# Batches 1 to 3 in stretches of 512 columns, and a new order of work behind the opening

## The chip, the cores and the metric

The kernel runs on one core of a Trainium2 chip. The metric is the device time of one execution in microseconds, as the median of several runs. The core has five engines that run side by side, each with its own queue of instructions in a fixed order: TensorE (PE in the profile; PEld is its loading of weights), VectorE (DVE), ScalarE (ACT), GpSimd (POOL), and SyncE (SP), which here only issues transfers.

## The reference

The input is q, k and v of four batches with four heads, 1088 positions and 32 features a head, two small matrices S1 and S2 of 8 x 32, and four weights. First comes an attention without softmax:

```
phi(x)  = outer(S1 x, S2 x) flattened to 64 features      (for every position and head)
kv      = sum over positions of phi(k) v^T                 (64 x 32)
z       = sum over positions of phi(k)
x       = phi(q) kv / (phi(q) z + 1e-6)                    (heads side by side: 1088 x 128)
```

Then two mixing steps, in float32 throughout:

```
h   = relu(x^T @ w_tok1) @ w_tok2        over positions: 1088 -> 256 -> 1088
u   = x + h^T
out = u + relu(u @ w_ch1) @ w_ch2        over channels:  128 -> 1536 -> 128
```

## The kernel before

**Splitting for accuracy.** A wide product of batches 1 to 3 and every channel product is made from three fast ones: each operand is cut into a high and a low part (`uh` and `ul`, `hh` and `hl`, the two `halves` of a weight), and high x high, high x low and low x high are added up in one PSUM bank. The weights arrive as 64-bit words that ACT, DVE and GpSimd turn into such halves in the opening.

**Stages.** For each batch b the keys' features and sums are made (`K<b>`: `.p` projects, `.c` copies, `.v` multiplies, `.s` sums over positions into a bank, `.kvz` copies that out). The queries' features are made by `Q<b>`; for batches 1 to 3 they go through DRAM (`.p`, `.c`, four writes `.w`, six broadcasting reads `.r`, then four multiplications `.m`). `A<b>` is the attention and the mixing over positions: `.x` the attention's matmuls (line 692), `.n`, `.r`, `.d` the division, `.h` and `.l` the split of x, `.t` the first product (line 758), `.relu`, `.hT` the transpose, `.w` the second product (line 878), `.xb`, `.xm` and `.xT` the transposition of x by way of DRAM, `.us` their sum u, `.uh` and `.ul` its split (lines 849 and 852).

**The channel mix.** All columns (positions of all batches, one after another) are cut into stretches, listed in `SPANS`: three for batch 0 and nine for batches 1 to 3, seven of 384 columns, one of 320 and one of 256. Stretch i has twelve blocks of 128 hidden channels. A block is four steps in the function `channel_mix`: `U<i>.f` (three matmuls into a bank of `ps_h`, line 928), `U<i>.h` (ACT's relu into `hh`, line 932), `U<i>.l` (DVE's low part into `hl`, line 935), and `U<i>.s` (three matmuls that add to the stretch's bank of `ps_o`, line 941). After the twelfth block `U<i>.ol` adds u (line 960 for batch 0, line 966 for the others) and `U<i>.out` stores the result from SP (line 977). A stretch that crosses from one batch to the next has two stores.

**The order.** Nothing is decided at run time. `ORDER` is a list of step names, written out by hand ahead of time; `Plan.run` emits the steps in that order, each into the queue of its engine (`@pool` and `@dve` choose one where there are several). `~n` stands for n matmuls on zeros that only keep PE occupied in the opening. Every step lies behind the earlier ones of its engine, and waits for the semaphores of what it reads.

**Buffers.** Each kind of tile rotates through a fixed number of buffers, given in `bufs` (line 223). The n-th tile of a kind takes buffer n modulo that number, once all readers of the tile that was there are done. Of the eight PSUM banks three are `ps_a`, three `ps_h` and two `ps_o`. `HID` = 4 buffers hold `hh` and `hl`, so that four blocks can stand between the first and the second product.

Of the kernel before, what the change touches and what calls it, by code (L numbers as in the profile page):

```python
# [89 lines left out]
w10.lo@pool U1.f U1.h U1.l U1.s U1.s w04.lo@pool U1.s A1.n0 U2.f U2.f k2 v2 A1.r0 A1.d0 q3 A1.n2 A1.r2 U1.h A1.n1  # L90
A1.r1 U1.l A1.d2 A1.d1 U1.s A1.xb A1.xm U2.f U2.h w11.hi U2.l K2.p U2.s k3 U2.h U2.l U2.h A1.xT0 K2.c0 K2.c8 U2.l
U2.f U2.f K2.c4 K2.v0 K2.v8 U2.s U2.f K2.v4 w14.lo@pool U2.s A1.xT1 A1.xT2 w12.hi Q2.p U2.h U2.h A1.h0 K2.s
w12.lo@dve A1.l0@pool U2.h Q2.c0 A1.h2 A1.h1 Q2.c1 A1.l2@dve A1.l1@dve U2.l Q2.w0 Q2.w3 w11.lo@dve w15.lo@dve K3.p
K2.kvz Q2.w2 A1.t0 U2.l U2.l U1.ol Q2.w1 K3.c4 A1.t1 A1.t2 K3.c0 A1.xT3 U2.s U1.out Q2.r0None K3.v0 U2.f Q2.r00
A1.relu A1.hT K3.v4 Q2.r01 U2.h Q2.r1None K3.c8 U2.l U2.s U2.f U2.h A1.hTh Q2.r10 U2.l U2.s U2.f U2.f A1.hTl Q2.r11
U2.f v3 U2.s U2.s K3.v8 A1.w0 U2.h U2.l U2.h U2.l A1.us0 U2.oh@dve U2.s A1.w1 A1.us1 A1.w2 A1.us2 U2.h U2.l A1.uh03
A1.uh14 U2.f U2.h U2.s U2.l A1.ul03@pool U3.f U2.s U3.f U3.f U3.h U3.l U3.f U3.h U3.l U2.s U3.s U3.f U3.h U3.h U2.ol
U3.l Q2.m00@dve U3.s U3.s U3.f U3.h U3.h A1.uh25 U3.l U3.s U3.f U3.h U3.l U3.f A1.ul25@pool U3.l U3.s U3.s U3.f U3.h
U3.l U3.h U3.f U3.s U3.h U3.l U3.l U3.f U3.l U3.h Q2.m01@dve U3.s U3.s U3.s Q2.m11@dve Q2.m10@dve U3.f U3.h U3.l
A1.ul14@pool U4.f U4.h A2.x A2.n2 A2.n0 U3.l U4.l A2.r0 A2.r2 A2.n1 U3.s A2.d0 A2.h0 U4.f U4.h U4.f A2.d2 A2.r1  # L100
A2.d1 A2.xb U4.l A2.l0@pool A2.h1 A2.xm K3.s A2.h2 A2.l2@dve Q3.p Q3.c0 Q3.c1 Q3.w0 Q3.w1 Q3.w3 Q3.w2 A2.l1@dve U3.s
U4.f U4.s A2.xT0 A2.xT1 U4.f A2.xT2 U4.s A2.xT3 U4.h U4.l U4.h Q3.r0None Q3.r00 Q3.r01 K3.kvz A2.t0 Q3.r1None Q3.r10
A2.t1 A2.t2 A2.relu U4.f U4.s U4.h A2.hT A2.hTh U4.l U4.l A2.hTl U4.f U4.s U4.s U4.h U4.l U4.f U4.f A2.w0 A2.w1 U4.h
U4.l U4.s U4.s U4.h U4.l U4.h U4.f U4.h U4.f U4.h A2.us0 A2.uh06 A2.uh05 A2.us1 U4.l U4.s A2.w2 A2.uh17 A2.uh16 U4.l
A2.ul05@pool U4.s U2.out A2.ul16@pool U4.f U4.h U5.f U4.s A2.us2 A2.uh27 A2.uh28 U4.l A2.ul06@pool U4.l U5.f U4.s
U5.f U4.s U5.h U5.h U5.l U5.f U5.h Q3.m00@pool U5.h Q3.r11 U5.l U3.ol U3.out U5.s U5.f U5.s U5.l U5.f U5.h U5.l U5.f
U5.l U5.f U5.s U5.s U5.s U5.h U5.l U5.f U5.h U5.l U5.f U5.s U5.s U4.ol U5.h U5.l U5.f U5.s U5.h U5.l U5.s
A2.ul17@pool U5.h U5.h U5.l U5.f U6.f U5.h U5.s U5.l U5.l Q3.m10@dve U6.f U5.s U5.s U6.f Q3.m11@pool U6.h U6.h
A2.ul27@dve U6.h U6.l U6.f Q3.m01@pool U6.h U6.s U6.l U6.l U6.s U6.f U6.h U6.f U6.h A3.x A3.n0 A3.n1 U6.l U6.l U6.l
U6.s A3.r1 A3.r0 A3.n2 A3.d0 A2.ul28@pool A3.h0 A3.d1 A3.l0@dve A3.h1 U6.s U6.s U5.ol U5.out U6.f U6.f U6.h U6.l  # L110
U6.f U6.s U6.s A3.r2 A3.d2 A3.h2 U6.f U6.h A3.xb U5.out A3.t0 A3.l2@dve A3.l1@pool U6.l U6.h A3.t1 U6.s U6.h A3.t2
U6.f U6.h A3.relu U6.l U6.f U6.s U6.h U6.l U7.f U6.s U6.l U6.l A3.hT A3.hTh U7.f U7.f U7.h A3.hTl U7.h U7.l U6.s
U6.s U7.f U7.l A3.w0 A3.w1 U7.f U7.s U7.s U7.h U7.h U7.h U7.l U7.l U7.s A3.w2 U7.f U7.h U7.f U7.s U7.h A3.xm A3.xT0
A3.xT1 A3.xT2 U7.l U7.f A3.xT3 A3.us0 A3.uh08 A3.ul08@pool A3.us1 U7.l U7.l U7.s A3.uh09 U7.f U7.s U7.f A3.uh110
U7.h A3.us2 U7.l U7.s A3.ul09@dve U7.h U7.l U7.s A3.ul110@dve A3.uh210 U7.f U7.f U7.h A3.ul210@dve U7.l U8.f A3.uh19
U7.s U7.s U7.h U7.l U7.s U8.f U7.h U7.l U8.h U8.h U8.l U7.s U8.f U4.out U6.ol U6.out U7.ol U7.out U8.h U8.l
A3.ul19@dve U8.s U8.f U8.h U8.s U8.f U8.h U8.l U8.l U8.f U8.f U8.s U8.l U8.s U8.f U8.s U8.h U8.h U8.h U8.l U8.s U8.f
U8.h U8.l U8.l A3.uh211 U8.s U8.f U8.f U8.s U8.l U8.f U8.h A3.ul211@pool U8.h U8.h U8.s U8.l U8.l U8.l U9.f U9.f
U9.f U8.s U8.s U8.s U9.h U9.l U9.h U9.l U9.h U9.s U9.f U9.h U8.ol U8.out U8.out U9.l U9.l U9.f U9.s U9.s U9.f U9.h
U9.h U9.s U9.f U9.l U9.f U9.l U9.s U9.f U9.s U9.h U9.h U9.h U9.l U9.f U9.s U9.l U9.h U9.s U9.f U9.h U9.l U9.f U9.l  # L120
U9.s U9.h U10.f U9.l U10.f U9.l U10.h U9.s U10.f U10.h U9.s U10.h U9.s U10.l U10.l U10.s U10.f U10.f U10.s U9.ol
U9.out U10.h U10.h U10.l U10.s U10.l U10.f U10.f U10.s U10.h U10.h U10.l U10.f U10.s U10.h U10.l U10.s U10.f U10.h
U10.l U10.f U10.s U10.h U10.l U10.f U10.h U10.l U10.l U10.f U10.s U10.l U11.f U10.s U10.s U10.h U10.l U11.f U10.s
# [96 lines left out]
def attn_mixer_kernel(ctx: ExitStack, tc: tile.TileContext, qT, kT, v1, s64, wt1, wt2, wc1, wc2, out):  # L220
    nc = tc.nc
    engines = {"dve": nc.vector, "pool": nc.gpsimd, "act": nc.scalar}
    bufs = {"c": 4, "tail": 4, "a_sb": 3, "ar": 3, "den": 2, "o_sb": 2, "q_sb": 2, "u": 4, "uh": 4, "ul": 4, "us": 2, "xb": 1, "xm": 2, "xT": 1, "rec": 2, "hid": HID, "hh": HID, "hl": HID, "rows": 2, "ps_a": 3, "ps_h": 3, "ps_o": 2}
# [201 lines left out]
    def keys(b, after, boost):  # L425
# [48 lines left out]
        def sums(p, t0, t1):  # L474
            def emit(_):
                if (p, t0) == (0, 0):
                    t["kv"] = bank("ps_a" if b else "ps_o")
# [11 lines left out]
            return emit
# [563 lines left out]
```

## Time and profile before

| | |
|---|---|
| time, median of 3 runs | 216.39 us (216.31 to 219.78) |
| the profiled execution's own time | 216.37 us |
| its span, first to last instruction | 213.9 us |
| PE busy | 209.5 us, 98% of the span, 1876 matmuls |
| DVE busy | 147.1 us, 69% |
| ACT busy | 116.2 us, 54% |
| GpSimd busy | 60.9 us, 28% |
| granted clock of TensorE | 1.00 in every stretch |
| transfers | 28.35 MB in all, mean 133 GB/s |

Busy time of PE counts from a matmul's start to its modelled end, and successive matmuls overlap, so the length of one row is no measure of what it costs; the distance between the starts of successive matmuls is. A wait is put down to the step that came last. The merged chain lists, in order of time, what the last instruction hung on, with the length that each piece takes on it.

### The profile page before, as it was taken

What the parts mean: (1) busy time and instruction counts of PE and PEld (TensorE: products, weight loads), DVE (VectorE), ACT (ScalarE), POOL (GpSimd) and SP (SyncE); (2) the same over time, 40 slices, a digit from 0 to 9 for tenths busy, and PEclk for the clock granted to TensorE, in tenths of its full rate; (3) what the DMA queues carried; (4) which work ended last, traced back from release to release, by engine and by line L of the source; (5) the groups of instructions that cost most, each with busy time, mean ns of one, the idle gap of its engine ahead of it and who ended that gap; (6) DMA issues with size and microseconds to landing.
All of it is one profiled execution on the core that took longest, in us unless ns stands there. A gap on an engine that the chain in (4) does not pass through costs nothing.

```text
span 213.9 us, 4865 instructions
## 1 busy us (share of the span) xinstructions
PE 209.5 (98%) x1876; PEld 199.1 (93%) x1876; DVE 147.1 (69%) x299; ACT 116.2 (54%) x282; POOL 60.9 (28%) x66
## 2 busy tenths in 40 slices
PE   8999999999999999999999999999999999999993
PEld 7779779999998999999999999999999999999993
DVE  2899999998789765777434666585547656556562
ACT  4788997988456245444344544443336453544541
POOL 3177686989971001301000660010000010000000
PEclk9999999999999999999999999999999999999999
DMA  6999985750778598300697400014400200100000
GB/s 223 402 405 409 399 328 129 138 146 10 241 304 242 148 193 171 135 3 3 203 221 184 123 29 0 3 37 142 120 0 0 78 0 0 37 3 37 0 31 25
DMA packets 11398, 28.35 MB, mean 133 GB/s; under 512 B 1520, under 2 KB 5616, under 8 KB 11376
## 3 DMA queue, kind: packets, MB, share of 16 engines
q1 hardware_dynamic: 11232, 27.79, 41.7%
q8 instruction: 14, 0.23, 0.5%
...
q14 instruction: 8, 0.07, 0.1%
...
## 4 chain that ended last, share of the span: by engine, by line
PE 97%; ACT 1%; DVE 0%; issue 0%
PE ps_o L941 34%; PE ps_h L928 33%; PE ps_a L758 5%; PE ps_a L692 4%; PE ps_a L878 4%; PE ps_o L264 3%; PE ps_a L483 3%; PE ps_a L436 2%; PE ps_a L874 2%; PE ps_a L752 1%; PE ps_a L574 1%; PE ps_o L483 1%; PE ps_a L629 1%; PE ps_h L574 1%; PE ps_a L783 1%; PE ps_a L792 1%
## 5 line engine op out<-in xcount | busy, mean ns | idle before, releaser
L935 DVE SCALAR_TENSOR_TENSOR hl<-ps_h,hh 128x384 fp32r<-128x384 f32 (+2 forms) x144 | 74.5, 531 | 46.0 <-ACT hh L932 45.3
L932 ACT ACTIVATE hh<-ps_h 128x384 fp32r<-128x384 f32 (+2 forms) x144 | 67.4, 474 | 63.1 <-PE ps_h L928 54.0
L928 PE MATMUL ps_h<-uh,halves 128*128 128x384 f32 (+2 forms) x288 | 85.4, 330 | 0.0
L941 PE MATMUL ps_o<-hh,halves 128*128 128x384 f32 (+2 forms) x288 | 71.2, 330 | 0.0
L928 PEld LDWEIGHTS ps_h<-uh,halves 128*128 128x128 f32 x288 | 53.1, 188 | 0.6
L941 PEld LDWEIGHTS ps_o<-hh,halves 128*128 128x128 f32 x288 | 50.2, 188 | 0.8 <-issue 0.4
L928 PE MATMUL ps_h<-ul,halves 128*128 128x384 f32 (+2 forms) x144 | 47.1, 327 | 0.0
L941 PE MATMUL ps_o<-hl,halves 128*128 128x384 f32 (+2 forms) x144 | 47.1, 327 | 0.0
L852 POOL TENSOR_TENSOR ul<-us,uh 128x320 fp32r<-128x320 f32 (+4 forms) x10 | 7.2, 727 | 71.1 <-ACT uh L849 71.1
L928 PEld LDWEIGHTS ps_h<-ul,halves 128*128 128x128 f32 x144 | 27.1, 188 | 0.2 <-DVE ul L852 0.2
L941 PEld LDWEIGHTS ps_o<-hl,halves 128*128 128x128 f32 x144 | 27.1, 188 | 0.0
L307 POOL TENSOR_TENSOR whole<-c,tail 128x512 int32<-128x512 int32 (+3 forms) x11 | 11.7, 1072 | 2.7 <-ACT tail L290 1.3
L286 ACT ACTIVATE c<-doubles 128x512 f32<-128x512 f32 (+3 forms) x17 | 10.5, 625 | 3.1 <-DMA doubles<-wt 2.5
L466 DVE TENSOR_TENSOR k_p<-ps_a,a_sb 128x1024 f32<-128x1024 f32 (+1 forms) x12 | 11.0, 947 | 0.0
L722 POOL TENSOR_TENSOR xl<-x,xh 128x384 fp32r<-128x384 f32 x3 | 3.0, 1014 | 26.0 <-ACT xh L718 26.0
L290 ACT ACTIVATE tail<-doubles 128x512 int32<-128x512 uint32 (+3 forms) x17 | 10.4, 625 | 0.0
L300 DVE SCALAR_TENSOR_TENSOR c<-doubles,ps_h 128x512 int32<-128x512 int32 (+3 forms) x17 | 10.3, 609 | 0.2
L297 DVE TENSOR_SCALAR ps_h<-c 128x512 int32<-128x512 int32 (+3 forms) x17 | 10.2, 613 | 0.1
L758 PE MATMUL ps_a<-halves,xh 128*128 128x256 f32 x54 | 9.8, 283 | 0.0
L692 PEld LDWEIGHTS ps_a<-kvz,qp 128*64 128x64 f32 x288 | 8.7, 138 | 0.9 <-issue 0.7
L692 PE MATMUL ps_a<-kvz,qp 128*64 128x66 f32 x288 | 9.3, 223 | 0.0
L264 PE MATMUL ps_o<-still 128*128 128x128 f32 x38 | 8.0, 364 | 1.1 <-DVE still L242 1.1
...
## 6 DMA issues: line engine op xcount, KB each, us to landing
...
```

The source lines that it names most:

```text
L264: nc.tensor.matmul(spare_ps[:, :P], lhsT=still, rhs=still, start=True, stop=True)
L286: nc.scalar.activation(f32(t["c"]), f32(high), AF.Abs)
L290: nc.scalar.activation(t["tail"], low.bitcast(U32), AF.Copy, scale=2.0 ** -29)
L300: nc.vector.scalar_tensor_tensor(t["c"], high, -(1 << 30), t["ps"], op0=ALU.bitwise_and, op1=ALU.bitwise_or)
L307: engines[e].tensor_tensor(dst(), t["c"], t["tail"], op=ALU.add)
L466: engines["pool" if on_pool else "dve"].tensor_tensor(t["k_p"][:pn, t0 * H:t1 * H], a.unsqueeze(3).broadcast_to([pn, n, R, R]), t["sb", t0 ...
L692: nc.tensor.matmul(x_ps[c:c + 64, o:o + 2 * (D + 1)], lhsT=qp[:, p, s0 + c:s0 + c + 64], rhs=kvz_all[b % 2][:, p, :2 * (D + 1)], start=Tru ...
L758: nc.tensor.matmul(t["h_ps"][:, :DTOK], lhsT=t[l][:m, i, :], rhs=part(0, piece, r, j * DTOK, DTOK)[:m], start=(i == 0 and k == 0), stop=(i ...
L928: nc.tensor.matmul(h_ps[:, :cn], lhsT=part(2, at[2][e][0], l, at[2][e][1] * P, P), rhs=r[:, :cn], start=(m == 0), stop=(m == 2))
L932: nc.scalar.activation(t["hh"][:, :cn], t["h"][:, :cn], AF.Relu)
L935: nc.vector.scalar_tensor_tensor(t["hl"][:, :cn], t["h"][:, :cn], 0.0, f32(t["hh"][:, :cn]), op0=ALU.max, op1=ALU.subtract)
L941: nc.tensor.matmul(outs[i][:, :cn], lhsT=part(3, at[3][e][0], l, at[3][e][1] * P, P), rhs=r[:, :cn], start=(e == 0 and m == 0), stop=(e == ...
```

## The change

The nine stretches of batches 1 to 3 become seven: five of 512 columns, one of 448 and one of 256. The tiles of a stretch are 512 columns wide in place of 384; `u`, `uh` and `ul` have three buffers in place of four. Batch 0's queries are loaded into a buffer of the kind `us`, and `q_sb` has one buffer in place of two. The sums of the keys of batches 2 and 3 go to a bank of `ps_o` in place of `ps_a`. The stores of stretches 3, 4 and 6 are cut by partitions into two, four and four pieces. `ORDER` is another list from batch 1's attention on; what stands ahead of that is the same.

```diff
-WIDE = 384
+WIDE = 512
...
-    for n in (384,) * 7 + (320, 256):
+    for n in (512,) * 5 + (448, 256):
...
+PIECES = {3: 2, 4: 4, 6: 4}
...
-    bufs = {..., "q_sb": 2, "u": 4, "uh": 4, "ul": 4, "us": 2, ...}
+    bufs = {..., "q_sb": 1, "u": 3, "uh": 3, "ul": 3, "us": 2, ...}
...
-        k_hold[b], q_hold[b], v_hold[b] = Hold("k_sb"), Hold("q_sb"), Hold("v_sb")
+        k_hold[b], q_hold[b], v_hold[b] = Hold("k_sb"), Hold("q_sb" if b else "us"), Hold("v_sb")
...
-            box["q_sb", 0] = new("q_sb", [P, S])
+            box["q_sb", 0] = new("us", [P, S])
...
-                    t["kv"] = bank("ps_a" if b else "ps_o")
+                    t["kv"] = bank("ps_a" if b == 1 else "ps_o")
...
-        kp_hold, kv_hold = Hold("k_p"), Hold("ps_a" if b else "ps_o")
+        kp_hold, kv_hold = Hold("k_p"), Hold("ps_a" if b == 1 else "ps_o")
...
-                    def store(_, i=i, b=b, c0=c0, m=m, d0=d0):
-                        nc.sync.dma_start(out[b][:, c0:c0 + m], outs["sb", i][:, d0:d0 + m])
+                    cuts = range(0, P + 1, P // PIECES.get(i, 1))
+
+                    def store(_, i=i, b=b, c0=c0, m=m, d0=d0, cuts=cuts):
+                        for p0, p1 in zip(cuts, cuts[1:]):
+                            nc.sync.dma_start(out[b][p0:p1, c0:c0 + m], outs["sb", i][p0:p1, d0:d0 + m])
```

From the new list, in order: batch 1's attention to its token products; the border of U2 and U3; the border of U3 and U4 with batch 2's attention ahead of it; batch 3's attention; and the end.

```diff
+w10.lo@pool U1.f U1.h U1.l U1.s U1.s w04.lo@pool U1.s A1.n0 U2.f U2.f k2 v2 A1.r0 A1.d0 A1.n2 A1.r2 U1.h A1.n1 A1.r1
+U1.l A1.d1 K2.p U2.h U2.h K2.c4 K2.c8 K2.c0 A1.d2 A1.xb A1.xm U2.l U2.l U2.f U2.f U2.h A1.h0 A1.l0@pool w12.hi A1.h2
+A1.h1 K2.v0 K2.v8 A1.l1@pool K2.v4 U1.s U2.s U2.f Q2.p q3 U1.ol k3 w15.lo@dve A1.xT0 A1.xT1 U2.s U2.l A1.l2@pool
+w11.hi A1.t0 A1.t1 w11.lo@dve A1.t2 A1.relu w12.lo@dve U2.h U2.h w14.lo@dve K2.s Q2.c0 Q2.c1 Q2.w0 K3.p K3.c8 K3.c4
...
+Q2.m10@pool A1.uh14 Q2.r10 Q2.r11 U2.l U2.l U2.s U2.s U2.f U3.f U2.s U3.f U2.h U2.l U2.s U3.h U3.h U3.l U3.f U3.f
+U3.h U3.h U2.ol U3.l U3.l U3.l U3.s U3.f U3.h U3.l U3.s U3.f U3.h U3.s U3.s U3.s U3.l A1.us2 A1.uh24 U3.f U3.f U3.h
+Q2.m11@dve U3.s Q3.p Q2.m01@dve K3.s Q3.c0 U3.l Q3.c1 A2.x U3.h U3.l A2.n0 A2.n2 U1.out U3.s U3.f U3.f A1.uh25 U3.s
+A2.r0 A2.n1 U3.f A2.r2 A2.d0 A2.h0 A2.l0@pool A2.t0 A2.r1 A2.d1 Q3.w0 Q3.w2 Q3.w3 Q3.w1 A2.h1 Q3.r0None Q3.r00 U3.h
+U3.h A2.l1@pool A1.ul24@pool A1.ul14@pool A2.t1 U3.h A2.d2 A2.xb A2.xm K3.kvz Q3.r01 Q3.m00@pool Q3.r1None Q3.r10
+A2.xT0 A2.xT1 A2.h2 U3.l U3.l U3.f U3.h U3.l U3.l U3.s U3.s U4.f U3.s U3.s U4.f U4.f U4.h U4.l U4.h A2.l2@dve A2.t2
+U4.f A2.relu Q3.r11 Q3.m01@pool A2.xT2 Q3.m10@pool Q3.m11@pool A2.xT3 A2.hT U4.h U4.h A2.hTh U4.l U3.ol U4.l U4.s
+U4.s U4.s A2.hTl A2.w0 A2.w1 A2.w2 U4.f U4.f U4.h U4.h A1.ul25@dve U4.l U4.f U4.l U4.s U4.s U4.l U4.f U4.s U4.f U4.h
+U4.h U4.l U4.s U4.l U4.h U4.f U4.h U4.s U4.f A2.us0 A2.us1 A2.uh05 A2.us2 A2.uh15 A2.ul15@dve A3.x U4.l U4.s U4.l
...
+U9.f U9.s U9.l U9.l U9.f U9.f U9.s U9.s U9.h U9.h U9.h U9.l U9.f U9.h U9.l U8.ol U8.out U9.l U9.l U9.s U9.s U9.s
+U9.s U9.ol U9.out
```

## Rows read from the trace of the kernel before

**Rows 1.** The page's busy times by engine, share of the span, instructions

```profile
PE 209.5 (98%) x1876; PEld 199.1 (93%) x1876; DVE 147.1 (69%) x299; ACT 116.2 (54%) x282; POOL 60.9 (28%) x66
```

**Rows 2.** The page's chain that ended last: by engine, by line

```profile
PE 97%; ACT 1%; DVE 0%; issue 0%
PE ps_o L941 34%; PE ps_h L928 33%; PE ps_a L758 5%; PE ps_a L692 4%; PE ps_a L878 4%; PE ps_o L264 3%; PE ps_a L483 3%; PE ps_a L436 2%; PE ps_a L874 2%; PE ps_a L752 1%; PE ps_a L574 1%; PE ps_o L483 1%; PE ps_a L629 1%; PE ps_h L574 1%; PE ps_a L783 1%; PE ps_a L792 1%
```

**Rows 3.** Windows: stretch, length, busy PE, PEld, DVE, ACT, POOL, clock, DMA

```profile
82.00:120.00 38.00, 38.00 (x360) 36.81 (x359) 23.08 (x47) 17.47 (x46) 5.25 (x7) 1.00 0.50 130
...
160.00:190.00 30.00, 30.00 (x175) 30.00 (x174) 18.55 (x39) 15.34 (x35) 1.21 (x2) 1.00 0.06 20
```

**Rows 4.** Waits of PE's matmuls: total us, times, longest us

```profile
PE ps_o L264 <- DVE still L242: 1.1, 1, 1.1
```

**Rows 5.** The merged chain, channel products: start us, length us, what, matmuls

```profile
163.51 1.56 PE ps_h L928 x9
...
189.51 0.52 PE ps_o L941 x3
190.03 0.88 PE ps_h L928 x6
...
193.34 0.88 PE ps_h L928 x6
...
200.38 0.35 PE ps_h L928 x3
...
203.55 0.71 PE ps_h L928 x6
...
209.21 1.43 PE ps_o L941 x12
```

**Rows 6.** Groups by form, weight loads: count, busy us, mean ns, idle before

```profile
L928 PEld LDWEIGHTS ps_h<-uh,halves 128*128 128x128 f32 x288 | 53.1, 188 | 0.6
```

**Rows 7.** Groups by form: ACT and DVE between the two products

```profile
L935 DVE SCALAR_TENSOR_TENSOR hl<-ps_h,hh 128x384 fp32r<-128x384 f32 x108 | 58.4, 553 | 37.2 <-ACT hh L932 36.5
...
L932 ACT ACTIVATE hh<-ps_h 128x384 fp32r<-128x384 f32 x108 | 52.4, 492 | 49.6 <-PE ps_h L928 43.0 <-PE ps_o L941 6.0
...
L935 DVE SCALAR_TENSOR_TENSOR hl<-ps_h,hh 128x320 fp32r<-128x320 f32 x24 | 11.2, 486 | 5.7 <-ACT hh L932 5.7
...
L932 ACT ACTIVATE hh<-ps_h 128x320 fp32r<-128x320 f32 x24 | 10.5, 437 | 9.1 <-PE ps_h L928 7.2 <-DVE hl L935 0.8 <-PE ps_o L941 0.6
```

**Rows 8.** Groups by form: the addition at the end of a 320-column stretch

```profile
L960 DVE TENSOR_TENSOR o_sb<-o_sb,ps_o 128x320 f32<-128x320 f32 x1 | 0.5, 489 | 0.4 <-PE ps_o L941 0.4
```

**Rows 9.** Groups by form: steps of batches that change engine

```profile
L672 POOL TENSOR_TENSOR qp<-qp,br 128x544 f32<-128x544 f32 x5 | 7.7, 1554 | 2.1 <-DMA br<-rows 2.1
...
L722 DVE TENSOR_TENSOR xl<-x,xh 128x384 fp32r<-128x384 f32 x6 | 3.1, 546 | 0.6 <-ACT xh L718 0.5
L722 POOL TENSOR_TENSOR xl<-x,xh 128x384 fp32r<-128x384 f32 x3 | 3.0, 1014 | 26.0 <-ACT xh L718 26.0
```

**Rows 10.** The merged chain: attentions of batches 1, 2 and 3

```profile
55.85 2.25 PE ps_a L692 x72
58.10 0.72 PE ps_h L928 x3
...
95.41 2.25 PE ps_a L692 x72
...
136.98 2.25 PE ps_a L692 x72
```

**Rows 11.** SP's timeline of transfers issued: start us, length us, line, what

```profile
65.43 1.28 SPq L826 DMA_DIRECT2D xT<-xm  x3
...
106.93 0.56 SPq L659 DMA_DIRECT2D qp<-rows  x1
...
110.52 0.60 SPq L662 DMA_DIRECT2D br<-rows  x1
```

**Rows 12.** SP's waits for additions; stores of line 977: ns min/median/max

```profile
SPq L977 <- DVE o_sb L966: 78.2, 7, 19.0
L977 SPq DMA_DIRECT2D outT<-o_sb x14: 332/357/441, 53.9 to 211.1; - x14
```

More of the change, by code (lines that the diff above doesn't have):

```diff
@@ L89 @@
 w13.hi U1.f U0.ol Q1.m10@dve U0.out A0.ul22 w13.lo@pool w02.lo@pool A1.x w01.lo@pool U1.l U1.h U1.l w14.hi q2
[L90 to L123, printed above, removed]
@@ L124 @@
-U11.f U11.h U11.h U11.h U11.l U11.l U10.s U11.s U11.f U11.f U11.s U10.ol U10.out U11.l U11.h U11.h U11.f U11.h U11.s
-U11.l U11.f U11.l U11.f U11.s U11.s U11.l U11.s U11.f U11.h U11.h U11.l U11.f U11.s U11.l U11.f U11.s U11.h U11.h
-U11.l U11.l U11.f U11.s U11.h U11.h U11.s U11.l U11.l U11.s U11.s U11.ol U11.out
+w10.lo@pool U1.f U1.h U1.l U1.s U1.s w04.lo@pool U1.s A1.n0 U2.f U2.f k2 v2 A1.r0 A1.d0 A1.n2 A1.r2 U1.h A1.n1 A1.r1
+U1.l A1.d1 K2.p U2.h U2.h K2.c4 K2.c8 K2.c0 A1.d2 A1.xb A1.xm U2.l U2.l U2.f U2.f U2.h A1.h0 A1.l0@pool w12.hi A1.h2
@@ new lines @@
+A1.h1 K2.v0 K2.v8 A1.l1@pool K2.v4 U1.s U2.s U2.f Q2.p q3 U1.ol k3 w15.lo@dve A1.xT0 A1.xT1 U2.s U2.l A1.l2@pool
+w11.hi A1.t0 A1.t1 w11.lo@dve A1.t2 A1.relu w12.lo@dve U2.h U2.h w14.lo@dve K2.s Q2.c0 Q2.c1 Q2.w0 K3.p K3.c8 K3.c4
+K3.c0 U2.l U2.l A1.xT2 Q2.w3 A1.xT3 A1.hT U2.s U2.f U2.h Q2.w1 Q2.w2 v3 K3.v0 A1.hTh U2.l A1.hTl U2.s U2.f U2.h
+K2.kvz U2.s U2.f U2.h U2.f U2.h A1.w0 K3.v4 U2.l U2.f U2.l U2.l K3.v8 A1.us0 U2.s U2.s A1.w1 A1.us1 A1.uh03 A1.uh13
+A1.ul13@pool U2.s U2.h A1.ul03@dve Q2.r0None U2.oh@dve U2.f U2.h A1.w2 Q2.r00 Q2.r01 Q2.r1None Q2.m00@pool
@@ new lines @@
+A2.xT0 A2.xT1 A2.h2 U3.l U3.l U3.f U3.h U3.l U3.l U3.s U3.s U4.f U3.s U3.s U4.f U4.f U4.h U4.l U4.h A2.l2@dve A2.t2
+U4.f A2.relu Q3.r11 Q3.m01@pool A2.xT2 Q3.m10@pool Q3.m11@pool A2.xT3 A2.hT U4.h U4.h A2.hTh U4.l U3.ol U4.l U4.s
+U4.s U4.s A2.hTl A2.w0 A2.w1 A2.w2 U4.f U4.f U4.h U4.h A1.ul25@dve U4.l U4.f U4.l U4.s U4.s U4.l U4.f U4.s U4.f U4.h
+U4.h U4.l U4.s U4.l U4.h U4.f U4.h U4.s U4.f A2.us0 A2.us1 A2.uh05 A2.us2 A2.uh15 A2.ul15@dve A3.x U4.l U4.s U4.l
+A2.ul05@pool U4.h A3.n0 A3.r0 A2.uh16 U4.f U5.f A2.ul16@dve U4.h A3.d0 A3.h0 A3.n2 U4.l U4.l A3.r2 A3.d2 U4.s U5.h
@@ new lines @@
+A3.n1 A3.r1 A3.d1 U5.l U4.s U5.f U5.f A2.uh26 A2.ul26@pool U5.h U5.l A3.l0@pool A3.h1 U4.s U5.f U5.f A3.t0 U5.s
+U3.out U2.out U5.h A3.h2 U5.h A3.l2@dve A3.l1@pool A3.t1 A3.t2 U5.s A2.uh27 A2.ul27@pool U5.l U5.f A3.relu A3.hT
+U5.s U5.l U5.h U5.l U5.h U5.f A3.xb A3.xm U5.s U5.f U5.s A3.xT0 A3.xT1 A3.xT2 A3.xT3 U5.l A3.hTh A3.hTl A3.w0 A3.w1
+U5.s U5.h U5.l U4.ol U4.out U5.f U5.f U5.s U5.h U5.h A3.w2 U5.l U5.f U5.s U5.h U5.l U5.l U5.f U5.s U5.h U5.h U6.f
+U6.h U5.s U5.l U5.s U5.l U6.f U5.s U6.l U6.f U6.f U6.s U6.h U6.l U6.f U6.s U6.h U6.l U6.f U6.h U6.h U6.h U5.ol U6.l
@@ new lines @@
+U6.f U6.l U6.f U6.s U6.s U6.h U6.s U6.l U6.f U5.out U5.out A3.us0 A3.us1 A3.uh18 A3.us2 A3.uh28 U6.l U6.s U6.s
+A3.ul28@dve U6.f A3.uh07 U6.h A3.ul07@pool U6.l U6.f U6.s U6.h U6.l U6.h U6.l U6.s U6.f U6.s U6.h U6.l U6.s U6.h
+U6.l U7.f U7.h U7.f U7.h U7.f U7.h U7.l U7.l U6.s U7.l A3.ul18@pool U6.ol U7.f U7.h U7.l U7.f U7.s U7.s U6.out U7.f
+U7.f U7.h U7.l U7.s U7.s U7.s U7.f U7.h U7.l U7.h U7.s U7.f U7.l U7.f U7.s U7.h U7.h U7.h U7.l U7.l U7.l U7.s U7.f
+U7.h U7.f U7.h U7.l U7.l U8.f U7.s U7.s U7.s U7.s U8.f U8.f U8.h A3.uh29 U8.l U8.f U8.s A3.ul29@pool U8.h U8.l U7.ol
@@ L127 @@
+U7.out U8.s U8.f U8.h U8.l U8.s U8.f U7.out U8.h U8.l U8.h U8.h U8.l U8.f U8.s U8.l U8.f U8.f U8.s U8.s U8.h U8.l
+U8.h U8.s U8.f U8.h U8.h U8.l U8.l U8.f U8.s U8.h U8.f U8.s U8.h U8.l U8.l U8.s U9.f U9.h U9.f U8.l U9.h U9.l U9.f
+U8.s U8.s U9.f U9.s U9.l U9.s U9.f U9.h U9.h U9.l U9.l U9.f U9.h U9.h U9.s U9.f U9.s U9.l U9.f U9.s U9.h U9.h U9.l
+U9.f U9.s U9.l U9.l U9.f U9.f U9.s U9.s U9.h U9.h U9.h U9.l U9.f U9.h U9.l U8.ol U8.out U9.l U9.l U9.s U9.s U9.s
+U9.s U9.ol U9.out
 """.split()
@@ L222, in attn_mixer_kernel @@
     engines = {"dve": nc.vector, "pool": nc.gpsimd, "act": nc.scalar}
-    bufs = {"c": 4, "tail": 4, "a_sb": 3, "ar": 3, "den": 2, "o_sb": 2, "q_sb": 2, "u": 4, "uh": 4, "ul": 4, "us": 2, "xb": 1, "xm": 2, "xT": 1, "rec": 2, "hid": HID, "hh": HID, "hl": HID, "rows": 2, "ps_a": 3, "ps_h": 3, "ps_o": 2}
+    bufs = {"c": 4, "tail": 4, "a_sb": 3, "ar": 3, "den": 2, "o_sb": 2, "q_sb": 1, "u": 3, "uh": 3, "ul": 3, "us": 2, "xb": 1, "xm": 2, "xT": 1, "rec": 2, "hid": HID, "hh": HID, "hl": HID, "rows": 2, "ps_a": 3, "ps_h": 3, "ps_o": 2}
     const = ctx.enter_context(tc.tile_pool(name="const", bufs=1))
```

## The prediction

> **What bounds the kernel now.** I read the page's busy times first: TensorE (PE) is busy for 98% of the span, DVE for 69%, ACT for 54% [rows 1]. Busy is not yet bound, so the chain that ended last comes next: 97% of it is PE, and two thirds are the two channel products of lines 928 and 941 [rows 2]. The windows show the same stage by stage: from 82 us to 120 us and from 160 us to 190 us PE is busy in every microsecond at a granted clock of 1.00, with DVE at about 60% [rows 3]. The waits that the profile puts down to PE's matmuls are one, of 1.1 us, at the very start [rows 4]. So no buffer, transfer or eviction is late behind the opening: what sets the end is how many matmuls PE issues and how far apart they start.
>
> That distance is read from the merged chain. From 163.51 to 190.03 us stand 153 matmuls of 384 columns: 26.52/153 = 173.3 ns. From 193.34 to 200.38 us stand 48 of 320 columns: 146.7 ns. From 203.55 to 209.21 us stand 48 of 256 columns: 117.9 ns [rows 5]. At 2.4 GHz, the upper of the clock's two levels, the columns alone take 160.0, 133.3 and 106.7 ns. Each matmul pays 13.3, 13.3 and 11.2 ns on top.
>
> **The change, part by part.** *Wider stretches.* Batches 1 to 3 have 3264 columns, before in 9 stretches (seven of 384, one of 320, one of 256), after in 7 (five of 512, one of 448, one of 256). A stretch costs 12 blocks x 6 matmuls = 72. So 648 matmuls become 504, over the same columns. Before: 504 x 173.3 + 72 x 146.7 + 72 x 117.9 ns = 106.4 us. After, with 13.3 ns on top of 213.3 and 186.7 ns: 360 x 226.7 + 72 x 200.0 + 72 x 117.9 = 104.5 us. The term is **-1.92 us**, all on the path, since PE never waits there.
>
> No row shows a 512-column matmul. The overhead grew by 2.1 ns from 256 to 384 columns; going on at that slope it would be 15.5 ns at 512 and 14.4 at 448, and the gain 1.07 us. If it fell back to the 11.2 ns of the 256 row, the gain would be 2.85 us. I take 13.3, the value of the two nearest rows, and keep 1.07 to 2.85 for the range.
>
> *The work between the two products.* ACT takes 492 ns for 384 columns and 437 for 320, DVE 553 and 486 [rows 7]; carried on by width, 512 columns take about 602 and 687 ns. PE spends 6 x 227 = 1360 ns on a block, so both engines keep up; the latency of a block (three matmuls, ACT, DVE) grows by some 0.4 us, and the four buffers that stand there already cover about three blocks. Price: 0 while the list keeps that distance.
>
> The Trainium skill speaks against wide pieces here: "Perfetto Trace Analysis", section "Optimizing Scalar/DVE Operations", says that where those engines cause bubbles on others, smaller instructions may let work finish sooner. It would bite only where PE waits for them, and the trace shows no such wait behind the opening; by it the time would be that of D below.
>
> *The bank of K2 and K3.* Their sums now come from the two-bank pool of the output sums. The takes then alternate U2 (bank 0), K2 (1), U3 (0), K3 (1), U4 (0): U3's first second-product needs U2's result read out, and U4's needs U3's. In the kernel before the neighbours had different banks. At the first border the new list puts two first-products of U3 (6 x 227 ns = 1.36 us) between U2's last matmul and U3's second product. DVE's addition for U2 takes 0.49 us [rows 8], starts about 0.2 us after PE has moved on, and is over at about 0.7 us; the DVE work ahead of it (the first block of U3, 0.69 us) can be done before U2's last matmul, since its first product stands two PE steps earlier. Margin some 0.6 us. At the second border three first-products, A2.t2 and the transpose stand between, 2.04 + 1.06 + 0.2 = 3.3 us (A2.t2 is nine matmuls of 117.9 ns); on DVE one xl (0.55 us) [rows 9], one block (0.69) and the addition (about 0.69 at 512) follow U3's end, behind an ACT step of 0.60: about 2.8 us. Margin 0.5 us. Price 0, and up to 0.5 us a border if DVE comes late.
>
> *The list behind the opening.* Two xl subtractions of batch 1 move from DVE (546 ns) to GpSimd (1014 ns) [rows 9]: A1.t2 may be ready up to 2 x 0.47 = 0.94 us later. Counted by hand, PE reaches it about 10 us after batch 1's attention, which ended at 58.10 us [rows 10], and GpSimd's third subtraction ends about half a microsecond earlier: 0, with 0.9 us as the other end. The attention of batch 3 moves forward, out of U6 into U4. Before, 136.98 - 97.66 = 39.3 us lay between the attentions of batches 2 and 3 [rows 10]; by the new list PE has 26.3 us of work there (29 first and second products x 0.68, the token products, w0 to w2). What must be done in it: the reads of the query features, which were issued within 106.93 to 111.12 us, about 4 us, in the kernel before [rows 11], then four products, now all on GpSimd, at 1.55 us [rows 9]. With r11 behind the xT reads on SP I get the last product about 20 us after the attention. Price 0, margin 6 us.
>
> *Queries.* Batch 0's go into a `us` buffer and `q_sb` has one. So q3 waits on SP for Q2.p, and k3 and xT0 queue behind it: xT0 goes out about 1.1 us later than at 65.43 us [rows 11]. By the same count xT3 lands just before A1.us0 wants it, and U3's first product comes 5 us after that. Price 0.
>
> *Stores.* 14 become 19 (two, four and four pieces for U3, U4, U6): five more at 0.36 us [rows 12], 1.8 us of SP. They hold back nothing but other stores and A3's move, and SP waited 78.2 us for these results [rows 12]. The last store has 256 columns as before, so the tail keeps its length.
>
> *Switches* between the narrow products (66 and 64 columns) and the wide ones cost about 0.2 us each: the three matmuls behind batch 1's attention took 0.72 where 0.52 is usual [rows 10]. Both lists have six of them behind the first difference. Price 0.
>
> Sum: the profiled execution took 216.37 us (span 213.9); 216.37 - 1.92 = **214.5 us**. It lies 0.02 us from the median of the runs, so nothing has to be shifted.
>
> **The rivals.** *A, the overhead is the weight load.* A weight load has a row of 188 ns [rows 6], longer than the 160 ns that 384 columns stream and shorter than the 213 ns of 512. If the 13.3 ns are the load sticking out, they vanish: 360 x 213.3 + 72 x 186.7 + 8.5 us = 98.7 us, a gain of 7.7 us, 208.7 us. Against it: at 256 columns the load would stick out by 81 ns, and the overhead there is 11.2 [rows 5]. Chance 0.03.
>
> The Trainium skill ("TensorE: Matmul & The Clock Gate", section "Back-to-back issue gap") gives columns/2.4 plus 2.5 ns for an isolated pair; by it a 512-column step would be an estimated 216 ns and the time some 210 us. The 13.3 ns of the 384 and 320 rows disagree with it.
>
> *B, the overhead is a share of the columns.* If it is 3.5% of the stream rather than a fixed piece, 512 columns take 231.1 ns and 448 take 202.2: 83.2 + 14.6 + 8.5 = 106.3 us, nothing gained, 216.2 us. For it: the rise from 11.2 to 13.3 ns between 256 and 320 columns. Against: none from 320 to 384. Chance 0.07.
>
> *C, short waits eat half.* The two borders and A1.t2 cost about 1 us together: 215.5 us. For it: margins of half a microsecond, counted by hand. Chance 0.13.
>
> *D, slower.* U4's bank. DVE reaches U3's addition late, because batch 2's divisions, its transposition and its xl subtractions fall into the same stretch as U3's 0.69 us blocks, and PE stands at U4's first second-product. It decides once the addition ends more than 2.4 us later than counted: the margin of 0.5 plus the whole gain. A backlog of five DVE blocks (3.4 us) would cost 2.9 us: 217.4 us. Against it: DVE has one block of 0.69 us per 1.36 us of PE. Chance 0.06.
>
> **How the numbers follow.** The forecast (gain 1.07 to 2.85, so 213.5 to 215.3, likeliest 214.5) gets 0.71. The range runs from 213.7 (about the lower end of the pitch's bounds) to 216.2 (which takes in C and most of B); outside stay A, D and slivers, about 0.13. A measurement of this kernel tells about 2%, 4.3 us, from no change. Only A goes beyond it downward: 0.03. Upward it takes a D of twice its size: 0.02. Within: 0.95.
>
> **What would show it.** The pitch: 36 matmuls of 512 columns should span 8.16 us; 7.7 is A, 8.3 is B. Chain: still 97% PE, lines 928 and 941 together about 1.9 us shorter. At the ends of U2 and U3 the chain should not pass through DVE's additions; if it does, C or D, and the piece of DVE in it is the price. The chain passing through A1.t2's GpSimd subtraction, or a DMA of batch 3's queries, would prove the margins of the list wrong. The forecast is wrong as a whole if PE shows waits in the windows behind 56 us.

## The result, and the profile after

The changed kernel takes 213.96 us in the median against 216.89 us of the kernel before beside it. The ratio is 0.9879 (0.9854 to 0.9904), which is 2.6 us less (2.1 to 3.2); it compares executions and is not the quotient of the two medians. Run twice more, beside the experiments below, the changed kernel gave ratios of 0.9917 (0.9883 to 0.9951) and 0.9845 (0.9799 to 0.9891). The forecast was 214.5 us, a gain of 1.9, with a range of 213.7 to 216.2. Two of its first 13 executions took 344 us at a mean granted clock of 0.56 and are left out of the ratio, and the profile shown here is that of its next run (its own time 214.62 us).

The page's busy times, and the chain that ended last by engine and by line. Line 926 is the first channel product now and 939 the second.

```profile
span 212.8 us, 4498 instructions
PE 208.2 (98%) x1732; PEld 181.7 (85%) x1732; DVE 140.4 (66%) x267; ACT 111.6 (52%) x257; POOL 68.2 (32%) x71
PE 94%; DMA 2%; ACT 1%; SPq 0%; issue 0%; DVE 0%
PE ps_h L926 34%; PE ps_o L939 33%; PE ps_a L756 4%; PE ps_a L876 4%; PE ps_a L690 4%; PE ps_o L481 3%; DMA us<-qT 2%; PE ps_a L434 2%; PE ps_a L872 2%; PE ps_a L750 1%; PE ps_o L262 1%; PE ps_a L572 1%; PE ps_a L481 1%; PE ps_a L627 1%; PE
```

Beside [rows 1, 2] the picture is the same with 144 fewer matmuls: PE at 98%, two thirds of the chain in the two channel products, DVE's additions 0% of it. PE has 94% of the chain and not the 97% that the prediction looked for, because 2% are the load of batch 0's queries in the opening, of which the change touches only the buffer. The waits of PE's matmuls, and the windows that answer to [rows 3, 4]:

```profile
PE ps_o L262 <- DVE still L240: 1.0, 1, 1.0
PE ps_a L572 <- DMA us<-qT: 0.4, 1, 0.4
```

```profile
82.00:120.00 38.00, 38.00 (x330) 32.68 (x329) 20.44 (x37) 15.71 (x36) 7.96 (x9) 1.00 0.67 152
160.00:190.00 30.00, 30.00 (x135) 24.93 (x134) 16.62 (x29) 14.32 (x27) 2.73 (x3) 1.00 0.04 10
```

Both waits lie in the first 7 us; behind the opening PE still waits for nothing, at a clock of 1.00. So the new time is again a count of matmuls times their distance. The merged chain gives that distance (start, length, what, matmuls), as [rows 5] did:

```profile
56.65 2.25 PE ps_a L690 x72
...
161.18 2.06 PE ps_o L939 x9
...
183.15 1.97 PE ps_h L926 x9
...
187.87 1.80 PE ps_h L926 x9
...
200.47 1.02 PE ps_h L926 x9
...
203.03 0.68 PE ps_o L939 x6
203.71 0.68 PE ps_h L926 x6
204.39 0.34 PE ps_o L939 x3
...
208.47 1.37 PE ps_o L939 x12
```

From 161.18 to 183.15 us stand 96 matmuls of 512 columns: 228.9 ns each. From 187.87 to 200.47 stand 63 of 448: 200.0 ns. The 15 of 256 columns from 203.03 to 204.73 take 113.3 ns; before it was 117.9 [rows 5]. On top of the columns at 2.4 GHz that is 15.5, 13.3 and 6.7 ns.

Between the two products, by form (count, busy, mean ns, idle before), as [rows 7]:

```profile
L933 DVE SCALAR_TENSOR_TENSOR hl<-ps_h,hh 128x512 fp32r<-128x512 f32 x60 | 40.7, 687 | 37.5 <-ACT hh L930 37.2
...
L930 ACT ACTIVATE hh<-ps_h 128x512 fp32r<-128x512 f32 x60 | 35.7, 599 | 45.7 <-PE ps_h L926 41.1 <-PE ps_o L939 2.3 <-ACT hTh L794 0.8
```

687 and 599 ns for 512 columns: the estimates from the rows of 320 and 384 columns were 687 and 602.

**Where the 1.75 us between the two profiled executions went** (216.37 to 214.62). From the start of batch 1's attention to the end of the last matmul PE took 154.79 us before (55.85 to 210.64) and takes 153.19 (56.65 to 209.84): -1.60. The opening ended 0.80 later. Over all profiles with batch 0's queries in a `us` buffer it ends between 55.93 and 57.03 us; for the kernel before there is one profile, so whether that buffer costs a few tenths there is not shown. From the last matmul to the end of the span it is 2.96 us in place of 3.26, and outside the span 1.82 in place of 2.47.

### The profile page after: what moved, and what is told of

The parts are those of the page before. It is cut to its first block, busy times and chain, and to the rows that moved or that the text cites. A ratio compares the mean times of both kernels' runs of the same rounds, so it can differ in the third digit from the quotient of the medians.

```text
span 342.1 us, 4498 instructions
## 1 busy us (share of the span) xinstructions
PE 337.9 (99%) x1732; PEld 236.8 (69%) x1732; DVE 146.1 (43%) x267; ACT 113.2 (33%) x257; POOL 67.5 (20%) x71
## 4 chain that ended last, share of the span: by engine, by line
PE 99%; DVE 0%; issue 0%
PE ps_h L926 35%; PE ps_o L939 34%; PE ps_a L756 5%; PE ps_a L876 4%; PE ps_a L690 4%; PE ps_o L481 3%; PE ps_o L262 3%; PE ps_a L434 2%; PE ps_a L750 2%; PE ps_a L872 2%; PE ps_a L481 1%; PE ps_a L572 1%; PE ps_h L572 1%; PE ps_a L627 1%; PE ps_a L781 0%; PE ps_a L790 0%
## 5 line engine op out<-in xcount | busy, mean ns | idle before, releaser
L933 DVE SCALAR_TENSOR_TENSOR hl<-ps_h,hh 128x512 fp32r<-128x512 f32 (+4 forms) x120 | 72.8, 609 | 151.5 <-ACT hh L930 151.4
L930 ACT ACTIVATE hh<-ps_h 128x512 fp32r<-128x512 f32 (+4 forms) x120 | 63.9, 534 | 162.7 <-PE ps_h L926 148.4
L926 PE MATMUL ps_h<-uh,halves 128*128 128x512 f32 (+4 forms) x240 | 116.2, 522 | 0.0
L939 PE MATMUL ps_o<-hh,halves 128*128 128x512 f32 (+4 forms) x240 | 102.2, 523 | 0.0
L939 PE MATMUL ps_o<-hl,halves 128*128 128x512 f32 (+4 forms) x120 | 62.2, 518 | 0.0
L926 PE MATMUL ps_h<-ul,halves 128*128 128x512 f32 (+4 forms) x120 | 61.8, 515 | 0.0
L926 PEld LDWEIGHTS ps_h<-ul,halves 128*128 128x128 f32 x120 | 27.0, 225 | 13.3 <-issue 6.6
L756 PEld LDWEIGHTS ps_a<-halves,xh 128*128 128x128 f32 x54 | 12.9, 278 | 1.4 <-issue 0.8
L670 POOL TENSOR_TENSOR qp<-qp,br 128x544 f32<-128x544 f32 x8 | 10.6, 1351 | 15.3 <-DMA br<-rows 15.3
L876 PE MATMUL ps_a<-halves,hTh 128*128 128x384 f32 (+1 forms) x36 | 13.3, 462 | 0.0
L481 PE MATMUL ps_o<-v_sb,k_p 128*64 128x66 f32 x216 | 11.4, 289 | 0.0
```

The source lines that it names most:

```text
L481: nc.tensor.matmul(t["kv"][j * F:(j + 1) * F, p * 2 * (D + 1):(p + 1) * 2 * (D + 1)], lhsT=t["k_p"][:n, i * H + h].rearrange("p i j -> p ( ...
L670: engines[e].tensor_tensor(qp[:, p, cs], qp[:, p, cs], t["br"][:, p, cs], op=ALU.mult)
L756: nc.tensor.matmul(t["h_ps"][:, :DTOK], lhsT=t[l][:m, i, :], rhs=part(0, piece, r, j * DTOK, DTOK)[:m], start=(i == 0 and k == 0), stop=(i ...
L876: nc.tensor.matmul(u_ps[:, :cn], lhsT=t[l][:, f, :], rhs=part(1, 2 * i + f, r, 0, cn), start=(k == 1), stop=(k == 6))
L926: nc.tensor.matmul(h_ps[:, :cn], lhsT=part(2, at[2][e][0], l, at[2][e][1] * P, P), rhs=r[:, :cn], start=(m == 0), stop=(m == 2))
L930: nc.scalar.activation(t["hh"][:, :cn], t["h"][:, :cn], AF.Relu)
```

## The experiments

**The changed kernel once more**, for its trace.

> The changed kernel itself, for a trace at the upper clock level. Theory (fixed piece of 13.3 ns per matmul): 36 matmuls of 512 columns span 8.16 us, the gain is 1.9 us, PE shows no wait behind the opening. Rival B (the overhead is a share of the columns): 8.3 us. Rival A (it vanishes): 7.7 us. If the gain is 2.6 us as first measured, the pitch theory leaves 0.7 us to be found: either on PE (narrow-to-wide switches, the opening) or outside the span.

Measured: 214.44 us, 0.9917. The trace is the one above.

**All stores whole.** The cut stores were costed at nothing.

```diff
-PIECES = {3: 2, 4: 4, 6: 4}
+PIECES = {}
```

> The changed kernel with every store in one piece again (14 of the cuts undone). Theory: SP has slack, so the time stays within 0.2 us of the changed kernel. Rival: the cut stores are part of the 0.7 us beyond the pitch; then the time rises by up to 0.7 us.

Measured: 214.04 us, 0.9892 (0.9849 to 0.9936), beside 214.44 of the changed kernel, with 2.0 and 2.4 us between the shortest and the longest execution of each. From batch 1's attention to the last matmul: 153.0 us against 153.2. The cut stores neither cost nor give anything that this tells, and they are not what makes the time outside the span shorter (1.79 us here too).

**Every 512-column matmul as two of 256 into the same bank.** It puts 360 matmuls back and leaves the list, the buffers and all other work as they are.

```diff
-nc.tensor.matmul(h_ps[:, :cn], lhsT=..., rhs=r[:, :cn], ...)
+for c0, c1 in ((0, 256), (256, 512)) if cn == 512 else ((0, cn),):
+    nc.tensor.matmul(h_ps[:, c0:c1], lhsT=..., rhs=r[:, c0:c1], ...)
...
```

The second product is cut in the same way.

> The changed kernel with each 512-column matmul issued as two of 256 columns into the same bank; list, tiles and evictions as they are, 360 matmuls more. Theory (fixed piece per matmul): 2 x 117.9 - 226.7 = 9.1 ns each, 360 x 9.1 = +3.3 us against the changed kernel, which is slower than the kernel before by about 1 us. Rival (the gain comes from the list, not from the number of matmuls): no more than 0.3 us.

Measured: 215.61 us, 0.9963 (0.9924 to 1.0002): 1.2 us more than the changed kernel beside it, which is neither the theory's 3.3 nor the rival's 0.3. From batch 1's attention to the last matmul it is 154.72 us, against 153.19 in the changed kernel and 154.79 in the kernel before: with the products cut, PE's gain is gone. Its merged chain:

```profile
124.49 0.68 PE ps_h L927 x6
125.17 2.25 PE ps_a L690 x72
...
128.33 1.41 PE ps_h L927 x12
...
159.40 2.12 PE ps_h L927 x18
...
186.16 2.72 PE ps_o L941 x24
```

A matmul of 256 columns has two levels: 0.68/6 = 113.3 ns ahead of batch 3's attention at 125.17 us, and 1.41/12 or 2.12/18 = 117.7 behind it. From 186.16, behind three matmuls of 448 columns, it is 2.72/24 = 113.3 again. The level changes where other matmuls stand between, and not within a run of such channel products. Against 228.9 ns for one of 512, two cost 6.5 ns more at the upper level and 2.2 ns less at the lower. So fewer matmuls is not a gain by itself: against the lower level of 256, the 512s win nothing. What a step costs on top of its columns is 6.7 or 11 ns at 256 and 15.5 at 512. Why the 256s have two levels stays open.

**Other widths, in the changed list.** Only the matmuls and ACT's and DVE's steps of U3 to U7 are narrowed. The columns left out get no channel mix; DVE copies u there.

```diff
+NARROW = {3: 504, 4: 496, 5: 480, 6: 464, 7: 432}
...
-            cn = sum(m for _, _, m in SPANS[i])
+            cn = NARROW.get(i, sum(m for _, _, m in SPANS[i]))
...
```

> The changed kernel with the channel products of stretches 3 to 7 over 504, 496, 480, 464 and 432 columns only; the rest of their columns is left out of the channel mix. For the pitch of a matmul at each width. If the piece on top is 13.3 ns up to 448 and grows with width beyond (15.5 at 512 by the changed kernel's trace): about 14 at 480, 15 at 504. If it is a step that belongs to a full 512-column bank: 13.3 at 504, 496, 480, 464 and 432, so 223.3, 220.0, 213.3, 206.7 and 193.3 ns.

Measured, in one execution: 209.31 us, span 207.5. The merged chain:

```profile
89.47 2.06 PE ps_o L941 x9
...
116.65 2.04 PE ps_h L928 x9
...
139.25 0.65 PE ps_o L941 x3
139.90 0.65 PE ps_h L928 x3
140.55 0.66 PE ps_o L941 x3
...
157.13 1.89 PE ps_h L928 x9
...
173.13 1.76 PE ps_o L941 x9
```

504 columns take 228.9 ns, as much as 512; 496 take 226.7, 480 about 218, 464 take 210.0 and 432 take 195.6. On top of the columns that is 18.9, 20.0, about 18, 16.7 and 15.6 ns. Both guesses of the expectation missed: 13.3 at all of them, and a rise from 13.3 at 448 over about 14 at 480 to 15 at 504. Rival B's share, 13.3/384 = 0.035 ns a column, would be 17.5, 17.2, 16.7, 16.1 and 15.0: near some of these, but it asks for 17.8 at 512 and 15.6 at 448, where 15.5 and 13.3 stand above.

The same with `NARROW = {3: 448, 4: 416, 5: 400, 6: 384, 7: 320}`:

> The same with 448, 416, 400, 384 and 320 columns in stretches 3 to 7 (the rest left out of the channel mix). Both theories: 13.3 ns on top at each, so 200.0, 186.7, 180.0, 173.3 and 146.7 ns. PE the bound throughout: the time falls below the changed kernel's by the columns left out over 2.4 GHz plus the change of the piece on top, 72 matmuls a stretch: about 72 x 5 x 229 - 72 x (200 + 186.7 + 180 + 173.3 + 146.7) ns = 18.6 us. Rival (a wait of the new list sets the end of a stretch): clearly less.

Measured, in one execution: 197.94 us, span 196.1: 16.5 us less than the changed kernel's 214.44, not 18.6. 384 and 320 columns cost here what they cost in the kernel before [rows 5], 1.56/9 = 173.3 and 1.32/9 = 146.7 ns, in the middle of another list:

```profile
152.68 1.56 PE ps_o L941 x9
...
163.91 1.32 PE ps_o L941 x9
```

By the starts of single matmuls 400 columns take about 181 ns and 416 about 189, which is 14 and 15 ns on top. So 320, 384 and 448 carry 13.3 ns, 512 carries 15.5, and 432, 464, 480, 496 and 504 more than either. Of the 2.1 us that are missing 1.4 are waits at batch 3's attention, which starts its halves 0.63 and 0.78 us late, by PE's timeline; the extra at 400 and 416 columns makes some 0.2, and the rest is not assigned. The halves, and then the merged chain ahead of them:

```profile
121.56 1.28 PE L692 MATMUL ps_a<-kvz,qp 128*64 128x66 f32 x36 [0.63 <-DVE us L894]
123.62 1.27 PE L692 MATMUL ps_a<-kvz,qp 128*64 128x66 f32 x36 [0.78 <-POOL qp L672]
```

```profile
106.80 12.63 DMA br<-rows
...
119.60 2.58 POOL qp L672 x2
122.21 1.37 POOL qp L672
```

With less work PE arrives early. The attention's first half waits for DVE's sums of batch 2, and its second half, the 36 matmuls from 123.62, hangs on a broadcasting read that lands 12.63 us after its issue and on GpSimd's products behind it, the last of which ends at 123.58.

**DVE's additions late.** Rival D said that U4's second product stands at DVE's addition for U3. Five small DVE additions (1.59 us) were put ahead of `U2.ol` and of `U3.ol`; they work on a tile of their own.

```diff
+    def linger(i):
+        if i in (2, 3):
+            for _ in range(5):
+                nc.vector.tensor_tensor(junk, junk, junk, op=ALU.add)
...
+                    linger(i)
                     nc.vector.tensor_tensor(outs["sb", i][:, :cn], ...)
...
```

> The changed kernel with five small additions on DVE (128 columns each, 0.28 us alone, some 1.0 to 1.4 us together) ahead of the read-out of U2 and again ahead of that of U3. Theory (margins of 0.6 and 0.5 us at the two borders): PE waits 0.4 to 0.9 us at each, +0.8 to +1.8 us in all. Rival (the borders are covered by more than I counted): under 0.3 us.

Measured: 215.41 us, 0.9923 (0.9888 to 0.9958). The median is 1.0 us above the changed kernel's beside it, which would suit the theory, but its ratio is only 0.0006 above the changed kernel's 0.9917, which is 0.1 us. From batch 1's attention to the last matmul it is 153.7 us, 0.5 more than without. Where, the timeline shows (start, length, engine, line, what), at U2's end and at U3's:

```profile
86.50 0.62 PE L947 MATMUL ps_o<-hh,halves 128*128 128x512 f32 x2
86.54 0.48 DVE L967 TENSOR_TENSOR o_sb<-o_sb,ps_o 128x320 f32<-128x320 f32 x1
...
86.93 1.88 DVE L941 SCALAR_TENSOR_TENSOR hl<-ps_h,hh 128x512 fp32r<-128x512 f32 x3
...
87.67 0.50 PE L934 MATMUL ps_h<-uh,halves 128*128 128x512 f32 x1 [0.32 <-DVE hl L941]
...
112.02 0.71 PE L947 MATMUL ps_o<-hh,halves 128*128 128x512 f32 x2
...
112.40 0.68 DVE L974 TENSOR_TENSOR o_sb<-us,ps_o 128x512 f32<-128x512 f32 x1
```

U3's second product starts at 86.50, before DVE has even begun to read U2's sums out at 86.54, and U4's at 112.02, before the addition at 112.40. Neither waited, so neighbours don't share a bank. With two banks that leaves one placing: U2 in one bank of `ps_o`, K2 and U3 in the other, K3 and U4 in the first again. U2's was still taken when U3 began, so U3 took the one that K2's sums had left. That fits a rule by which a tile takes the buffer that has been free longest, in place of number n modulo the count; the rule itself was not tested. What PE did wait for is an `h` bank, 0.3 us, because DVE's low parts stand in line behind the added work.

**The small edits without the new list.** The kernel before, its stretches of 384 and its own list, with batch 0's queries in a `us` buffer, one `q_sb`, and the cut stores. With one `q_sb` the load q3 has to stand behind `Q2.p`, and k3 follows q3 as in the changed kernel.

```diff
-... A1.r0 A1.d0 q3 A1.n2 ... K2.p U2.s k3 U2.h ... w12.hi Q2.p U2.h ...
+... A1.r0 A1.d0 A1.n2 ... K2.p U2.s U2.h ... w12.hi Q2.p q3 k3 U2.h ...
...
```

> The kernel before, with 384-column stretches and its own list, plus two small edits of the change: batch 0's queries in a us buffer with one q_sb buffer (the loads of q3 and k3 moved behind Q2.p), and the stores of stretches 3, 4 and 6 in two, four and four pieces. Theory: no price, within 0.3 us of the kernel before, and the time outside the span stays at its 2.1 us. Rival: these edits are what shortens the time outside the span from 2.1 to 1.8 us.

Measured: 223.07 us, 1.03 (1.0219 to 1.038). A miss. The chain, PE's timeline at the wait, and the windows (as [rows 3]) around it:

```profile
67.77 5.45 DMA k_sb<-kT
...
74.76 4.71 PE ps_a L760 x27
```

```profile
73.35 1.40 PE L438 MATMUL ps_a<-s_blocks,k_sb 128*64 128x64 f32 x36 [3.86 <-DMA k_sb<-kT]
```

```profile
69.00:73.00 4.00, 0.50 (x18) 0.35 (x13) 2.73 (x7) 0.42 (x2) 0.00 (x0) 1.00 0.96 330
73.00:82.00 9.00, 8.65 (x82) 8.55 (x83) 2.85 (x3) 1.80 (x7) 0.00 (x0) 0.81 0.76 187
84.00:120.00 36.00, 36.00 (x349) 34.81 (x349) 21.75 (x43) 15.18 (x38) 3.88 (x4) 1.00 0.41 110
```

k3 is issued at 67.77 and lands 5.45 us later; in the old list `K3.p` stands right there and PE waits 3.86 us for it. Behind the wait the granted clock is 0.81 in the mean until 82 us, between its two levels (1.2 and 2.4 GHz), and `A1.t` takes 4.71 us for 27 matmuls that take 3.07 in the changed kernel. From batch 1's attention to the last matmul it is 160.3 us in place of 154.8. The new list has `A1.t0` to `A1.t2` and `K2.s` ahead of `K3.p`, 5.3 us of PE's work. Without that the small edits together cost 6.6 us (223.07 against 216.46), and the wait for k3 is where it begins. PE's path explains 5.5 of them; k3 ahead of q3 was not tried in the old list, so that the late k3 is the whole cause is argued, not shown.

**k3 ahead of q3**, in the changed kernel, with the changed kernel itself beside it.

```diff
-... U2.f Q2.p q3 U1.ol k3 w15.lo@dve ...
+... U2.f k3 Q2.p q3 U1.ol w15.lo@dve ...
...
```

> The changed kernel with batch 3's keys (k3) loaded ahead of batch 3's queries (q3): SP issues k3 as soon as K2.p is through, about 63.3 us, in place of 66.9. Theory (the edge is only an edge): in the changed kernel k3 was issued at 66.92 and K3.p started without a wait at 72.34, 5.42 us later; a k3 load that was waited for took 5.45 us. So the load lands just in time, and taking it 3.6 us forward gains 0 to 0.1 us: median within 0.3 us of the changed kernel run beside it, and K3.p still at about 72.3. Rival (the edge costs in the executions that are about 2 us longer, 216.2 in place of 214.0): K3.p waits there, as it did 0.5 us in the narrower kernel; then the long executions become rarer or end near 215, and the mean falls by 0.5 us or more.

> The changed kernel once more, beside the one with k3 first on the same chip. Every theory: 213.9 to 214.5 us, channel pitch 228.9 ns at 512 columns, no wait of PE's matmuls behind the opening.

Measured: 213.85 us with k3 first and 213.96 without, ratios 0.9856 (0.9795 to 0.9917) and 0.9845 (0.9799 to 0.9891). SP's timeline and the merged chain, with k3 first:

```profile
64.07 0.37 SPq L266 DMA_DIRECT2D k_sb<-kT  x1
66.89 0.33 SPq L266 DMA_DIRECT2D q_sb<-qT  x1
```

```profile
72.72 1.05 PE ps_a L434 x36
```

And without, on the same chip:

```profile
66.29 0.38 SPq L266 DMA_DIRECT2D k_sb<-kT  x1
```

```profile
71.70 1.22 PE ps_a L434 x36
```

`K3.p` follows `K2.s` without a wait in both, and takes 0.17 us less when its keys are there early. From batch 1's attention to the last matmul it is 153.00 against 153.17 us. That is what the late load costs: a little more than the theory's 0 to 0.1. The expectation was wrong on the narrowed kernel: its wait of 0.5 us for keys lies in the opening, at 9.02 us, and not at `K3.p`. An execution 2 us above the others (216.05) came with k3 first, and none of six without, so the rival is not borne out.

## Why the prediction was right, and where it was not

**The mechanism held.** Behind the opening PE waits for nothing, DVE's additions are not in the chain, and what moved is the number of matmuls times their distance. No engine and no transfer took the place of PE, and the time fell inside the range. The split products show it from the other side. Added up by the distances of their starts, the channel products from batch 1's attention on take some 121.0 us before, 119.4 in the changed kernel and 121.1 with the products split, and PE's stretch there is 154.79, 153.19 and 154.72 us: the new list by itself takes nothing off PE's path that these profiles tell.

**Wider stretches: the term was mis-sized.** It had 13.3 ns on top of 512 columns as on top of 320 and 384. The trace has 15.5, the end that came from going on at the slope between 256 and 384 columns. With the measured distances, 360 x 228.9 + 72 x 200.0 + 72 x 113.4 = 105.0 us in place of 106.4: -1.46 us, where -1.92 was forecast and a gain of 1.07 was the lower bound. Of the -1.46, 0.32 come from the last stretch, whose 256s run at their lower level now; the prediction held them at 117.9. PE's stretch from batch 1's attention to the end shortened by 1.60, so 0.14 are unassigned. The narrowed kernels show that the piece on top is not in order of width at all, so the slope gave 15.5 by chance: no line through the three rows of before could have given it for a good reason. Why the piece is what it is at each width stays open.

**The sum came close by terms that it did not have.** Against the forecast gain of 1.9 the three ratios make 2.6, 1.8 and 3.4. PE's path gives 1.6, which by itself would have been 214.8 us and inside the range too. The time outside the span gives 0.3 to 0.5 more: its median over 29 executions of the kernel before is 2.08 us and over the ten beside the last two kernels 2.31, over 50 of the changed kernel and its variants 1.78 to 1.80. It is not the number of instructions (5211 with the split matmuls, 1.79) nor the cut stores (1.79 without). The old list with the small edits keeps 2.04 (four executions), so it seems to go with the new list or its stretches; how stays open. From the last matmul to the end of the span 0.3 more are seen, in one pair of profiles. The rest was not found. Beside the last two kernels the spans of the kernel before ran from 213.6 to 216.3 us and those of the changed one from 212.1 to 212.2, but in its two earlier runs from 211.5 to 214.5; no profile shows where the longer executions lose their time.

**The bank of K2 and K3: the step failed, at price 0 by luck.** It said that takes alternate and that U3's and U4's second products wait for their neighbour's read-out with margins of 0.6 and 0.5 us. The late additions show that they wait for nothing of the kind. The sentence on buffers that both steps rest on, n modulo the number, does not hold for `ps_o` in this program. Rival D named a place where nothing could happen; DVE in arrears costs PE through the `h` banks instead, 0.3 us for 1.59 us of added work.

**The list behind the opening.** `A1.t2` was right: the third subtraction on GpSimd ends 0.7 to 0.8 us before PE needs it (0.5 forecast). This is GpSimd's timeline, and the merged chain for `A1.t` and for batch 3's attention:

```profile
66.08 2.25 POOL L720 TENSOR_TENSOR xl<-x,xh 128x384 fp32r<-128x384 f32 x2 [0.23 <-ACT xh L716]
...
119.76 4.04 POOL L670 TENSOR_TENSOR qp<-qp,br 128x544 f32<-128x544 f32 x3 [7.22 <-DMA br<-rows]
```

```profile
67.02 3.07 PE ps_a L756 x27
...
125.61 2.25 PE ps_a L690 x72
```

The 27 matmuls from 67.02 run without a gap; the last nine begin at about 69.1, GpSimd ends at 68.33. But batch 3's attention (136.98 before [rows 10]) was said to have a margin of 6 us, with the last product 20 us after batch 2's attention. It comes 24.7 us after it, at 123.80, and PE begins at 125.61, with the second half at about 126.7: a margin of 1.8 to 2.9. The prediction reckoned with reads that take about 4 us to issue, and not with their landing; the last one went out at 107.68, and GpSimd's last three products began some 12 us later, at 119.76. Price 0 all the same, but the narrowed kernel waits 1.4 us right there.

**Queries: 0, but not for the reason given.** The step looked at xT0, which went out at 67.40 in place of 65.43 [rows 11] (0.80 of it is the later opening) and held nobody up. It named k3 as queued behind q3 and gave it no price. That was the edge: k3 is issued at 66.92 and `K3.p` starts at 72.34, 5.42 us later, where such a load took 5.45. In the old list with the small edits PE waits 3.86 us for it, in the new one its lateness costs 0.2.

**Stores: 0**, as said: 19 of 413 ns in the median, 0.36 us forecast for each [rows 12], and whole ones no faster.

**The rivals.** A (the weight load sticks out) wanted 7.7 us for 36 matmuls of 512; it is 8.24. The Trainium skill's figure of 2.5 ns on top for an isolated matmul (the page "TensorE: Matmul & The Clock Gate", section "Back-to-back issue gap") is not what this stream of matmuls with a weight load each shows: 15.5 at 512 columns. B wanted 8.3 for the 36 and nothing gained; 448 columns carry no more than 320, and the channel products alone gained 1.46 us. At 512 by itself it was as near as the forecast, 231.1 against 226.7 for the 228.9 measured. (What the prediction called 3.5% of the stream is 0.035 ns a column, 8% of the stream; its numbers are worked out from that.) C (short waits eat half) would have put waits into PE's list, which has none behind the opening. D is answered above.
